# First-block decays spread by TensorE, arithmetic taken off GpSimd, raw weights held back

## The chip, the cores and the metric

One core of a Trainium2 chip runs the whole program. The metric is the time of one execution on the device in microseconds, the median over several runs. The profile is of one further execution.

## The reference

Three stages follow one another. The first is a chunked scan over 768 positions for 4 batches x 8 heads (head size 32, state size 16), in float32:

```python
for c in range(nc):
    cum = np.cumsum(la, axis=-1)                       # la = log(clip(a, 1e-6, 1))
    L = np.exp(cum[:, :, :, None] - cum[:, :, None, :]) * causal
    y_intra = np.einsum('bhij,bhjd->bhid', np.einsum('bhin,bhjn->bhij', Cc, Bc) * L, xc)
    y_inter = np.einsum('bhin,bhnd->bhid', Cc, state) * np.exp(cum)[:, :, :, None]
    y[:, :, sl] = y_intra + y_inter
    state = decay_full[:, :, None, None] * state + np.sum(Bx, axis=2)
```

Then come two MLPs over the 3072 tokens of width 256: an RMS norm and `silu(xn @ w_gate) * (xn @ w_val) @ w_out` with 1536 hidden columns, and `g @ w_out` with `h = x @ w_in`, `g = h * clip(h + 3, 0, 6) / 6` and 2048 hidden columns. The weights arrive as 64-bit floats.

## The kernel before

The tokens are cut into six blocks of 512. Stage A runs the first MLP over blocks j = 0 to 5 in twelve steps f each, stage B the second over six blocks in sixteen steps each. A step has a hidden part (`hidden`, products named hps), a gate on ACT, a product with it on DVE (`prod`, L793 or L795, which also frees the PSUM that the next hidden part needs), a split of the result into a high and a low part (`hi` on ACT, `lo`), and a result part (`result`, products named acc). Every matrix product is made of three products of rounded float32 operands (`mm3`, L752), 18 of 512 columns in a step of A and 12 in one of B. `lo` is a subtraction that runs on GpSimd (POOL) or DVE: `either` (L244) leaves the choice to the planner, and `two` (L247, instructions at L248) issues it.

The scan is done in 24 chunks k of 128 positions and one batch, in pairs q; block j needs the chunks 4j to 4j+3. For a pair, `load` (L341) brings `cb` (B, C, x), `L` (the decay factors, broadcast over 64 partitions) and `P` (their running products) in by DMA. `scan` (L400, DVE) makes the lower triangle of decays out of L, `bh` and `ch` scale B and C; PE makes scores (`score`, L426) and state updates (`grow`, L437); DVE multiplies scores by decays (`decay`, L480, tile SM), masks (`um`) and carries the state (V); PE makes y (`intra`, L451, and `inter`, L460). `finish_chunk` squares y and copies it out (ACT). The chunks of block 0 (pairs 0 and 1) come first; `norm_pair` (L557) then takes their means (PE, L537), a square root (ACT), a reciprocal and a Newton step (DVE), sends the result back through PE (L574), scales x and splits it into xh and xl. Later pairs are worked in `visit`s put between the steps of stage A at places given by `AT`; a visit does the front of a new pair and the back (y) of the one before it. `norm` (L612) does the same for later blocks, with a trip through DRAM (rnd, rb). For pair 0, L comes from the raw input and is clipped on DVE (L368); for the others it comes from `azero`, the clipped copy that `prefixes` (L300) writes to DRAM.

`weights` (L687) loads a raw weight tile, puts the two halves of its 64-bit numbers together (ACT L703 and L708, DVE `join` L712), and splits it into wh (ACT or DVE) and wl (POOL or DVE). Six raw buffers exist.

The order on every engine comes from `Plan` (L34): operations with a cost per engine, dependences, and a priority (the longest tail behind it plus a boost) are list-scheduled in model time, and the instructions are issued in that order. Each engine, and SP's queue of DMA issues, works in order. `Plan.run` also puts dummy products of zeros (`idle`, L310) into PE's gaps from the opening of the MLP's PSUM up to the first step.

Of the kernel before, what the change touches and what calls it, by code (L numbers as in the profile page):

```python
# [30 lines left out]
AT = [[2, 6, 8]] + [[0, 5, 6]] * 4  # L31


class Plan:  # L34
# [48 lines left out]
    def run(self):  # L83
# [32 lines left out]
        while len(out) < len(ops):  # L116
# [18 lines left out]
            if not now[e]:  # L135
# [4 lines left out]
            soon = min((r for r, s in future[e] if r < t + self.WAIT and s not in done  # L140
                        and -tail[s] - ops[s][4] < pri - self.MARGIN), default=None)
# [45 lines left out]
def block_kernel(ctx, tc, comb, ablk, w1, w2, cst, out):  # L187
# [8 lines left out]
    att, early, mlp = ExitStack(), ExitStack(), []  # L196
# [17 lines left out]
    rawx = [ap1.tile([128, 1536], F32, name=f"rawx{f}") for f in range(NRAW - 3)]  # L214

    P = Plan({"L": 2, "cb": 2, "P": 2, "ch": 4, "bh": 2, "SM": 4, "um": 4, "V": 6, "V1": 4,
              "S": 1, "S0": 1, "xT": 1, "sq": 1, "rn": 1, "rb": 1, "x": 2, "p": 3, "gh": 3,
# [8 lines left out]
    def dma(nbytes, n=1, e="DMA"):  # L226
        return {e: max(560 * n, nbytes // 300) if e == "DMA" else 560 * n, "bytes": nbytes}
# [4 lines left out]
    def d1(n):  # L232
        return 72 + 1.04 * n
# [10 lines left out]
    def either(n):  # L244
        return {"DVE": d1(n), "POOL": g1(n)}
# [14 lines left out]
    def setup():  # L260
        dve.memset(zero, 0.0)
        dve.memset(ones, 1.0)
        dve.memset(half, 0.5)
        pool.memset(eye8, 0.0)
# [54 lines left out]
    def place(k):  # L319
        return ("S0", 0) if 2 <= k < B else ("S", k // 2 - (k >= B))  # L320

    def bank4(k):
        p = ps_0 if 2 <= k < B else ps_at
        if p not in T:
            T[p] = p.tile([128, 4, 512], F32, name="sps")
        return T[p]
# [13 lines left out]

    def load(q):  # L341
        k0, bst = 2 * q, BOOST if 2 * q >= B else BOOST0 + (3000 if q == 0 else 0)
# [645 lines left out]
```

## Time and profile before

| | us |
|---|---|
| median of 3 runs (642.71 to 643.81) | 643.24 |
| the profiled execution | 643.43 |
| its span, first to last instruction | 641.6 |
| PE busy | 608.3 (95%) |
| DVE busy | 311.2 (49%) |
| ACT busy | 293.9 (46%) |
| POOL busy | 282.1 (44%) |

Busy times are unions of the instructions' durations; a matmul's record is longer than its distance to the next, since they are pipelined. Matmuls of plain float32 operands stand in the trace as two records each. An arrow in brackets names what ended an engine's idle time before an instruction.

### The profile page before, as it was taken

The page shows a single profiled execution, that of the slowest core. Times are in us where ns is not written, and L with a number is a line of the kernel's source. Part 1 is how long each engine was busy: PE and PEld are TensorE (multiplying, and loading weights), DVE is VectorE, ACT ScalarE, POOL GpSimd, SP SyncE. Part 2 cuts the span into 40 slices and gives each one's busy share as a digit, 9 for nine tenths or more (in the row PEclk, how much of TensorE's full clock was granted, in tenths as well). Part 3 has the DMA queues.
Part 4 walks back from the last instruction along what each step waited for, and adds up shares of the span by engine and source line. Part 5 has one row for each costly group of instructions (what it writes and reads, how often), then busy time and mean ns, then how long its engine had stood idle before and what let it go on. Part 6 is the DMA issues. An engine that isn't in the chain of part 4 may idle for free.

```text
span 641.6 us, 10828 instructions
## 1 busy us (share of the span) xinstructions
PE 608.3 (95%) x4414; PEld 491.9 (77%) x4414; DVE 311.2 (49%) x474; ACT 293.9 (46%) x484; POOL 282.1 (44%) x245
## 2 busy tenths in 40 slices
PE   1689999999999999999999999999999999999997
PEld 0567777778777777777888878788788787888886
DVE  4589975771683366255666422422424224222223
ACT  1368743232323233335766344545454454545443
POOL 3255373353334235233544344545455454544443
PEclk9999999999999999999999999999999999999999
DMA  7977314300340220022433000000000000000000
GB/s 254 313 241 287 102 32 129 105 18 1 100 111 7 79 79 17 3 83 76 140 131 113 0 1 0 1 33 2 1 34 1 0 34 1 5 29 1 33 1 33
DMA packets 15817, 42.18 MB, mean 66 GB/s; under 512 B 2116, under 2 KB 5400, under 8 KB 15768
## 3 DMA queue, kind: packets, MB, share of 16 engines
q1 hardware_dynamic: 15064, 39.63, 19.3%
q10 hardware_dynamic: 704, 1.87, 0.8%
q8 instruction: 34, 0.56, 0.4%
q14 instruction: 15, 0.12, 0.1%
HBM read 38.14 MB, written 3.35 MB: 65 GB/s over the span
## 4 chain that ended last, share of the span: by engine, by line
PE 78%; DVE 11%; DMA 5%; issue 4%; SPq 1%; ACT 0%; POOL 0%; DVEq 0%; POOLq 0%
PE hps L752 43%; PE acc L752 31%; DMA rb<-rnd 2%; DVE p L793 1%; DVE z L551 1%; DVE xT L648 1%; PE sps L451 1%; PE sps L460 1%; DVE xl L248 1%; DVE xh L254 1%; DVE yT L712 1%; DMA pref<-ac 1%; PE sps L426 1%; DVE y L552 1%; DMA rnd<-y 1%
## 5 line engine op out<-in xcount | busy, mean ns | idle before, releaser
L248 POOL TENSOR_TENSOR gl<-p,gh 128x512 fp32r<-128x512 f32 x161 | 215.5, 1338 | 300.0 <-ACT gh L800 279.7
L800 ACT CAST gh<-p 128x512 fp32r<-128x512 f32 x168 | 104.7, 623 | 117.2 <-PE acc L752 115.2
L795 DVE SCALAR_TENSOR_TENSOR p<-p,hps 128x512 f32<-128x512 f32 x96 | 65.9, 687 | 175.9 <-ACT p L787 175.8
L787 ACT ACTIVATE p<-hps,half 128x512 f32<-128x512 f32 x96 | 66.0, 687 | 76.9 <-POOL gl L248 76.2
L752 PE MATMUL hps<-xh,w1h 128*128 128x512 f32 x288 | 91.2, 398 | 4.4 <-DVE p L793 3.7
L752 PE MATMUL hps<-xh,w1l 128*128 128x512 f32 x288 | 89.4, 392 | 0.0
L752 PE MATMUL hps<-xl,w1h 128*128 128x512 f32 x288 | 89.2, 391 | 0.0
L793 DVE TENSOR_TENSOR p<-p,hps 128x512 f32<-128x512 f32 x72 | 49.1, 681 | 64.7 <-PE hps L752 56.3
L785 ACT ACTIVATE p<-hps 128x512 f32<-128x512 f32 x72 | 43.0, 598 | 79.4 <-POOL gl L248 66.2
L752 PE MATMUL acc<-gh,w2h 128*128 128x512 f32 x192 | 74.7, 389 | 0.0
L752 PE MATMUL acc<-gl,w2h 128*128 128x512 f32 x192 | 74.7, 389 | 0.0
L752 PE MATMUL acc<-gh,w2l 128*128 128x512 f32 x192 | 74.7, 389 | 0.0
L752 PEld LDWEIGHTS hps<-xh,w1h 128*128 128x128 f32 x288 | 53.1, 190 | 19.2 <-DVE p L793 6.8
L752 PEld LDWEIGHTS hps<-xh,w1l 128*128 128x128 f32 x288 | 54.4, 189 | 11.7
L752 PEld LDWEIGHTS hps<-xl,w1h 128*128 128x128 f32 x288 | 54.4, 189 | 11.6
L752 PE MATMUL hps<-xh,w2h 128*128 128x512 f32 x192 | 59.7, 392 | 2.1 <-DVE p L795 2.1
L752 PE MATMUL hps<-xh,w2l 128*128 128x512 f32 x192 | 59.2, 389 | 0.0
L752 PE MATMUL hps<-xl,w2h 128*128 128x512 f32 x192 | 59.1, 389 | 0.0
L752 PE MATMUL acc<-gh,w1h 128*128 128x512 f32 x144 | 57.4, 399 | 0.9 <-issue 0.9
L752 PE MATMUL acc<-gh,w1l 128*128 128x512 f32 x144 | 56.1, 390 | 0.0
L752 PE MATMUL acc<-gl,w1h 128*128 128x512 f32 x144 | 56.1, 390 | 0.0
L752 PEld LDWEIGHTS hps<-xh,w2h 128*128 128x128 f32 x192 | 35.6, 188 | 11.3 <-DVE p L795 4.3
(98 smaller groups left out, 710.4 us busy)
## 6 DMA issues: line engine op xcount, KB each, us to landing
cb<-comb SPq DMA_DIRECT2D x10, 896.0 KB
raw<-w SPq DMA_DIRECT2D x16, 512.0 KB
L<-azero SPq DMA_DIRECT2D x22, 256.0 KB
yT<-w SPq DMA_DIRECT2D x6, 768.0 KB
rawx<-w SPq DMA_DIRECT2D x6, 768.0 KB
out<-yT SPq DMA_DIRECT2D x12, 256.0 KB
P<-pref SPq DMA_DIRECT2D x24, 64.0 KB
rb<-rnd SPq DMA_DIRECT2D x5, 256.0 KB
```

Source lines behind the costliest of these rows:

```text
L248: eng[e].tensor_tensor(out=out, in0=a, in1=b, op=op)
L254: dve.tensor_copy(out, a)
L426: pe.matmul(out=o[64 * c:64 * c + 64, p], lhsT=cb[r, BN + c * SC:BN + (c + 1) * SC], rhs=cb[r, CP + c * CH:CP + (c + 1) * CH], start=True, ...
L451: pe.matmul(out=y[32 * g:32 * g + 32, 2 * t + c], rhs=SM[r, h], lhsT=cb[r, XX + D * h:XX + D * h + D], start=first, stop=True, skip_group_ ...
L460: pe.matmul(out=y[q:q + 64, p // 2 * 2 + c], lhsT=before(k, c)[r, :], rhs=T["ch", k][r, SC * c:SC * c + SC], start=False, stop=True, skip_ ...
L551: dve.tensor_tensor(out=z, in0=z, in1=y, op=ALU.mult)
L752: pe.matmul(out=o, lhsT=a, rhs=c, start=first and i == 0, stop=last and i == len(seq) - 1)
L785: act.activation(out=p[:, :n], in_=hid(hs[0])[:, :n], func=AF.Silu)
L787: act.activation(out=p[:, :n], in_=hid(hs[0])[:, :n], func=AF.Relu, scale=1.0 / 6.0, bias=half)
L793: dve.tensor_tensor(out=p, in0=p, in1=h, op=ALU.mult)
L795: dve.scalar_tensor_tensor(out=p, in0=p, scalar=1.0, in1=h, op0=ALU.min, op1=ALU.mult)
L800: act.copy(out=t[:, :n], in_=T["p", i][:, :n])
```

## The change

- The decays of chunks 0 to 3 no longer come by DMA. `ex` multiplies the clipped decays (96 rows, 256 columns) by stationaries of 128 columns that hold ones in one row pair (`pick`, copied on ACT out of the unit matrix); the product in PSUM (`Q`) is the broadcast, which the scan reads directly. `px` does the same for the running products of the second half chunk, which ACT copies into P (`back`). The raw decays for that arrive in a fifth group of columns of `ac`.
- Three products of zeros (`heat`: 512, 512 and 256 columns) stand first on PE; `idle` is now 512 columns wide and is put into gaps from the last mean of block 0 on.
- No subtraction or scaling goes to POOL: `either` names DVE alone.
- Raw weight f is held until another has landed: POOL copies one column into its buffer first, reading um of chunk 1 (f = 1) or an earlier raw weight (f from 2).
- Block 0's pairs are put in a new order: scores and updates of a pair together, y of both chunks in one piece (`first`), squares ahead of the means and copies behind; the root reads PSUM, xh is made in two parts. PSUM for pair 1 (`open0`) takes the banks of `Q` when all four scans have read them.
- The visits of blocks 0 and 1 are put at other steps (`VISITS`): pair 4 moves from block 0 to block 1, and pair 3's y stands alone.
- Up to the first step the planner waits longer for a more urgent operation (`calm`), and it takes DMA to run at 370 instead of 300 bytes per ns.

```diff
-AT = [[2, 6, 8]] + [[0, 5, 6]] * 4
+NWARM = (4, 4, 2)
+VISITS = {0: [(0, 2, None), (2, 3, 2), (6, None, 3), (8,)],
+          1: [(0, 4, None), (3, 5, 4), (6, 6, 5), (7,)]}
...
+            ahead, margin = self.WAIT, self.MARGIN
+            if i < self.calm:
+                ahead, margin = max(ahead, 0.6 * ops[i][0][e]), 1000
+            soon = min((r for r, s in future[e] if r < t + ahead and s not in done
+                        and -tail[s] - ops[s][4] < pri - margin), default=None)
...
-            t = 1 + next(s for s, i, _, _ in out if i == after)
+            t = 1 + max(s for s, i, _, _ in out if i in after)
...
+    ps_q = early[0].enter_context(tc.tile_pool(name="ps_q", bufs=1, space=PSUM))
+    Q = [ps_q.tile([128, 512], F32, name=f"spread{i}") for i in range(4)]
...
-        return {"DVE": d1(n), "POOL": g1(n)}
+        return {"DVE": d1(n)}
...
+        dve.memset(ac[:, 4], 1.0)
...
+    def four(t, n=4):
+        return t.rearrange("p (o n) -> p o n", o=1).to_broadcast([128, n, 128])
+
     def idle():
-        if "idle" not in T:
-            T["idle"] = mlp[0].tile([128, 512], F32, tag="acc0", name="idle")
-        pe.matmul(out=T["idle"][:, :128], lhsT=zero, rhs=zero, start=True, stop=True)
+        pe.matmul(out=bank4()[:, 0], lhsT=zero, rhs=four(zero), start=True, stop=True)
...
+    def heat(e):
+        for n in NWARM:
+            pe.matmul(out=Q[3][:, :128 * n], lhsT=zero, rhs=four(zero, n), start=True, stop=True)
+
+    spread = []
+
+    def broadcast():
+        def ex(e, k):
+            for u in range(2):
+                pe.matmul(out=Q[k][:, 256 * u:256 * u + 256], rhs=flat(az[:, :4]),
+                          lhsT=pick[:, 2 * k + u].rearrange("p c n -> p (c n)"),
+                          start=True, stop=True)
+
+        def px(e):
+            for k in range(B):
+                pe.matmul(out=Q[3][:, SC * k:SC * k + SC], rhs=ac[:32, 4],
+                          lhsT=eyeN[:, H * k:H * k + H].rearrange("p h n -> p (h n)"),
+                          start=True, stop=True, skip_group_check=True)
+
+        def back(e, q):
+            copy(e, tile2("P", q, [CH])[:, :, SC:],
+                 Q[3][:, 128 * q:128 * q + 128].rearrange("p (k i) -> p k i", i=SC))
+
+        def each(e):
+            act.copy(out=eyeN, in_=eye[:32, :32].rearrange("p (r n) -> p r n", n=1)
+                     .to_broadcast([32, 32, N]))
+
+        def spot(k):
+            for u in range(2):
+                r = 2 * k + u
+                act.copy(out=pick[:, r:r + 1], in_=eye[:96, :96].rearrange("p (c m o) -> p m c o", c=2, o=1)
+                         [:, r:r + 1].to_broadcast([96, 1, 2, SC]))
+
+        P.op({"ACT": 2 * a1(128)}, lambda e: spot(0), r=[("eye", 0)], w=[("raw", 4)], boost=4e5)
+        P.op({"ACT": 2 * a1(128)}, lambda e: spot(1), r=[("eye", 0)], w=[("pick", 1)], boost=3e5)
+        for k in (2, 3):
+            P.op({"ACT": 2 * a1(128)}, lambda e, k=k: spot(k), r=[("eye", 0)], w=[("pick", k)],
+                 boost=1e5)
+        P.op({"PE": 4500}, heat, w=[("hot", 0)], boost=1e9)
+        P.op({"ACT": a1(512)}, each, r=[("eye", 0)], w=[("raw", 5)], boost=2e5)
+        def some(k, bst):
+            P.op({"PE": 800}, lambda e, k=k: ex(e, k), w=[("Lp", k)],
+                 r=[("az", 0), ("raw", 4)] + ([("pick", k)] if k else []), boost=BOOST0 + bst, seq=[("Su", 0, 1)] if k == 3 else [])
+
+        some(0, 6000)
+        some(1, 6000)
+        P.op({"PE": 800}, px, r=[("ac", 0), ("raw", 5)], w=[("Lp", 3)], boost=BOOST0 + 5000)
+        for q in range(2):
+            P.op({"ACT": a1(128)}, lambda e, q=q: back(e, q), r=[("Lp", 3)], w=[("P", q)],
+                 boost=BOOST0 + 5000)
+        spread.append(lambda: [some(k, 0) for k in (2, 3)])
...
-                    in_=(azero if q else ablk)[c, k0:k0 + 2].rearrange("k m -> (k m)")
+                    in_=azero[c, k0:k0 + 2].rearrange("k m -> (k m)")
...
-        def clip(e, k):
-            t = T["L", k]
-            dve.tensor_scalar(out=t, in0=t, scalar1=1e-6, scalar2=1.0, op0=ALU.max, op1=ALU.min)
-            dve.memset(t[:, :, 0:1], 0.0)
-
-        seq = {1: [("P", 0)], 2: [("raw", 2)]}.get(q, [])
         cbs, Ls = [("cb", q, i) for i in range(2)], [("L", q, i) for i in range(2)]
+        seq = [("raw", 2)] if q == B // 2 else []
         if q == 0:
-            P.op(dma(98304), lambda e: nc.sync.dma_start(out=ac, in_=rows(ablk)), w=[("ac", 0)],
-                 boost=1e6)
-            P.op(dma(524288, 2), ld_L, w=Ls, boost=9e5)
-            for i in range(2):
-                P.op(dma(458752, 1, "ACT"), lambda e, i=i: ld_cb(e, i), w=[cbs[i]], boost=8e5)
+            P.op(dma(8192, 1, "ACT"), lambda e: act.dma_start(
+                out=ac[:32, 4], in_=ablk[1, :B].rearrange("k (h i) -> (k h) i", i=SC)),
+                w=[("ac", 1)], boost=2e6)
+            P.op(dma(98304), lambda e: nc.sync.dma_start(out=ac[:, :4], in_=rows(ablk)),
+                 w=[("ac", 0)], boost=1e6)
...
+            broadcast()
+        if q < B // 2:
+            for i, e in enumerate(("ACT", "DMA")):
+                P.op(dma(458752, 1, e), lambda e, i=i: ld_cb(e, i), w=[cbs[i]],
+                     boost=8e5 - 1e5 * q)
+        if q >= B // 2:
+            P.op(dma(524288, 2), ld_L, r=[("azero", 0)], w=Ls, boost=bst, seq=seq)
+            P.op(dma(917504), ld_cb2, w=cbs, boost=bst, seq=seq)
+            P.op(dma(131072, 2), ld_P, r=[("pref", 0), ("pref", 1)], w=[("P", q)], boost=bst)
 
 
         def scan(e, k):
+            if k < B:
+                tile2("L", q, [H, SC])
             L = flat(T["L", k])
-            dve.tensor_tensor_scan(out=L, data0=L, data1=flat(eye8), initial=0.0,
-                                   op0=ALU.mult, op1=ALU.add)
+            dve.tensor_tensor_scan(out=L, data0=Q[k] if k < B else L, data1=flat(eye8),
+                                   initial=0.0, op0=ALU.mult, op1=ALU.add)
...
+                 r=[("eye", 0), Ls[i] if k >= B else ("Lp", k)], w=[Ls[i]], boost=bst,
+                 seq=[("x", 0, 1, 2)] if q == B // 2 else [])
+            P.op(either(128) if k >= B else {"DVE": d1(128)}, lambda e, k=k: bh(e, k), r=[cbs[i], Ls[i]], w=[("bh", k)], boost=bst)
...
-            act.activation(out=rn(0)[2][:, k0:k0 + 2], in_=rn(0)[0][:, k0:k0 + 2], func=AF.Sqrt)
+            act.activation(out=rn(0)[2][:, k0:k0 + 2], in_=pair(k0)[:, :, 0], func=AF.Sqrt,
+                           scale=1.0 / DM, bias=eps)
...
-        def hi(e):
-            copy(e, parts()[0], T["xT", 0][:, :, cols])
+        def hi(e, t):
+            copy(e, parts()[0][:, t], T["xT", 0][:, t, cols])
...
+        if hold:
+            P.op({"POOL": 200}, lambda e: hold[0](raw(f)), r=hold[1], w=[kr], boost=soon, seq=seq)
...
+        P.op({"DVE": d1(cols)} if soon else either(cols), lo, r=[kt if wide else kr, kh], w=[kl],
+             boost=bst)
...
+    def open0(e):
+        early[0].close()
+        ps_0 = early[1].enter_context(tc.tile_pool(name="ps_0", bufs=1, space=PSUM))
+        T["ps", 1] = ps_0.tile([128, 4, 512], F32, name="sps0")
...
-            P.fill = idle, 225, opened[0], 4000, len(P.ops)
+            P.calm = len(P.ops)
+            P.fill = idle, 900, warm, 4000, len(P.ops)
...
+    def first(ks):
+        for k in ks:
+            intra(k)
+        pe.drain()
+        for k in ks:
+            inter(k)
+        pe.drain()
+
+    load(0)
     for q in range(2):
-        load(q)
-        for k in (2 * q, 2 * q + 1):
-            r, w = front_keys(k)
-            P.op({"PE": 700}, lambda e, k=k: score(k), r=r[:1], w=w[:1], boost=BOOST0)
-            P.op({"PE": 500}, lambda e, k=k: grow(k), r=r + w[:1], w=w[1:], boost=BOOST0)
+        ks = [2 * q, 2 * q + 1]
+        for k in ks:
+            rf, wf = front_keys(k)
+            P.op({"PE": 350}, lambda e, k=k: score(k), r=rf[:1] + [("open0", 0)][:q], w=wf[:1],
+                 boost=BOOST0 + 3000, seq=[] if q else [("Lp", k)])
+        for k in ks:
+            rf, wf = front_keys(k)
+            P.op({"PE": 250}, lambda e, k=k: grow(k), r=rf, w=wf[1:], boost=BOOST0 + 3000,
+                 seq=[("Sc", q, 1)])
+        if q == 0:
+            spread[0]()
+            load(1)
+            P.op({"HOST": 0}, open0, r=[("L", n, i) for n in range(2) for i in range(2)] +
+                 [("P", n) for n in range(2)], w=[("open0", 0)])
+    for q in range(2):
+        ks, r, w = [2 * q, 2 * q + 1], [], []
+        for k in ks:
             middle(k)
-        for k in (2 * q, 2 * q + 1):
-            r, w = back_keys(k)
-            P.op({"PE": 700}, lambda e, k=k: (intra(k), inter(k)), r=r, w=w, boost=BOOST0)
-            finish_chunk(k)
...
-        norm_pair(q, 0)
+            r, w = r + back_keys(k)[0], w + back_keys(k)[1]
+        P.op({"PE": 1500}, lambda e, ks=ks: first(ks), r=r, w=w, boost=BOOST0)
+        norm_pair(q, 0, [finish_chunk(k) for k in ks])
+    P.op({"HOST": 0}, open1, r=[("xT", 0, 2, t) for t in range(2)] + [("um", k) for k in (2, 3)],
+         w=[("open", 1)])
+    warm = last_mean[-1:]
...
+    def hold(f):
+        g = max(f - 2, 0) + (f == 2)
+
+        def go(t):
+            s = flat(T["um", 1]) if f == 1 else raw1(g)[:, 1:]
+            pool.tensor_copy(t[:, :1], s[:, :1])
+
+        return (go, [("um", 1) if f == 1 else ("raw", g)]) if f else ()
...
+                seq=[("azero", 0)], hold=hold(f))
+
+    def visit(q, o):
+        new, old = [[] if n is None else [2 * n, 2 * n + 1] for n in (q, o)]
...
-            if j == 0 and f == 0:
-                visit(B // 2)
-            if f in AT[j][:2]:
-                visit((j + 1) * B // 2 + 1 + AT[j].index(f))
-            if f == AT[j][2]:
+            n = 2 * j + 3
+            for v in VISITS.get(j, [(0, n, n - 1), (5, n + 1 if n + 1 < NK // 2 else None, n), (6,)]):
+                if v[0] == f and len(v) == 3:
+                    visit(*v[1:])
+            if f == VISITS.get(j, [(6,)])[-1][0]:
```

## Rows read from the trace of the kernel before

**Rows 1.** Windows: length, busy PE, PEld, DVE, ACT, POOL, clock, DMA share, GB/s.
```profile
7.00:37.00 30.00, 14.52 (x286) 11.42 (x287) 18.01 (x39) 11.89 (x22) 8.17 (x11) 1.00 0.97 291
37.00:91.00 54.00, 51.85 (x587) 40.40 (x587) 50.43 (x66) 37.74 (x60) 29.42 (x26) 1.00 0.49 170
91.00:148.00 57.00, 55.95 (x555) 44.77 (x554) 37.60 (x65) 17.04 (x31) 25.20 (x25) 1.00 0.25 75
```

**Rows 2.** Waits of PE from 40 us on: total us, times, longest.
```profile
PE hps L752 <- DVE p L793: 3.7, 7, 0.8
```

**Rows 3.** Timeline of the start, pair 0: start, us, engine, line, operation.
```profile
4.57 0.69 DVE L293 TENSOR_TENSOR_SCAN ac<-az,ah 96x256 f32<-96x256 f32 x1
...
12.93 0.69 DVE L480 TENSOR_TENSOR SM<-sps,L 128x512 f32<-128x512 f32 x1 [0.83 <-PE sps L437]
...
14.94 0.48 DVE L486 TENSOR_TENSOR um<-sps,gs 128x128 f32<-128x128 f32 x2
...
15.47 0.68 PE L451 MATMUL sps<-SM,cb 64*32 64x64 f32 x32 [1.24 <-DVE um L486]
...
17.11 0.49 PE L460 MATMUL sps<-ch,um 32*64 32x64 f32 x8
```

**Rows 4.** The same timeline, pair 1.
```profile
17.80 2.34 DVE L400 TENSOR_TENSOR_SCAN L<-L,eye 128x512 f32<-128x512 f32 x2 [1.13 <-DMA L<-azero]
...
27.36 0.49 PE L460 MATMUL sps<-ch,um 32*64 32x64 f32 x8
```

**Rows 5.** The same timeline, from y to the first product.
```profile
29.16 1.86 PE L537 MATMUL sps<-ones,sq 128*128 128x1 f32 x8 [0.17 <-ACT xT L252]
...
31.24 1.53 DVE L712 SCALAR_TENSOR_TENSOR yT<-yT 128x768 int32<-128x768 int32 x1
...
33.50 1.22 PE L574 MATMUL sps<-eye,y 128*128 128x128 f32 x4 [2.47 <-DVE y L552]
...
35.78 1.62 PE L313 MATMUL idle<-zero 128*128 128x128 f32 x6 [1.06 <-DVE xT L579]
...
37.05 1.20 PE L752 MATMUL hps<-xh,w1h 128*128 128x512 f32 x2
```

**Rows 6.** The same timeline, scores of a pair before and after the first product.
```profile
21.06 1.16 PE L426 MATMUL sps<-cb 32*64 32x128 f32 x32
...
41.32 0.69 PE L426 MATMUL sps<-cb 32*64 32x128 f32 x32
```

**Rows 7.** The same timeline, pairs of products of 512 columns.
```profile
38.05 1.05 PE L752 MATMUL hps<-xh,w1l 128*128 128x512 f32 x2
...
38.90 1.05 PE L752 MATMUL hps<-xl,w1h 128*128 128x512 f32 x2
...
44.29 0.62 PE L752 MATMUL hps<-xh,w1l 128*128 128x512 f32 x2
...
44.75 0.62 PE L752 MATMUL hps<-xl,w1h 128*128 128x512 f32 x2
```

**Rows 8.** The same timeline, DVE and POOL side by side.
```profile
43.57 4.44 DVE L400 TENSOR_TENSOR_SCAN L<-L,eye 128x512 f32<-128x512 f32 x2
...
44.18 2.75 POOL L248 TENSOR_TENSOR w1l<-yT,w1h 128x768 fp32r<-128x768 f32 x1
```

**Rows 9.** Groups: DVE 0 to 37 us; DVE, POOL 37 to 91: busy, mean ns.
```profile
L400 DVE TENSOR_TENSOR_SCAN L<-L,eye 128x512 f32<-128x512 f32 x5 | 5.9, 1210 | 1.2 <-DMA L<-azero 1.1
...
L400 DVE TENSOR_TENSOR_SCAN L<-L,eye 128x512 f32<-128x512 f32 x7 | 12.0, 1747 | 0.0
...
L248 POOL TENSOR_TENSOR gl<-p,gh 128x512 fp32r<-128x512 f32 x9 | 14.3, 1585 | 18.3 <-ACT gh L800 12.8 <-DVE w1l L248 5.5
L248 POOL TENSOR_TENSOR w1l<-yT,w1h 128x768 fp32r<-128x768 f32 x3 | 6.5, 2151 | 1.8 <-ACT w1h L252 1.8
L248 POOL TENSOR_TENSOR bh<-cb,L 128x128 f32<-128x128 f32 x7 | 5.4, 774 | 5.9 <-DVE L L400 5.9
```

**Rows 10.** Timeline, a subtraction of 512 columns on DVE by itself.
```profile
36.68 0.67 DVE L248 TENSOR_TENSOR xl<-xT,xh 128x512 fp32r<-128x512 f32 x1
```

More of the change, by code (lines that the diff above doesn't have):

```diff
@@ L226, in dma @@
     def dma(nbytes, n=1, e="DMA"):
-        return {e: max(560 * n, nbytes // 300) if e == "DMA" else 560 * n, "bytes": nbytes}
+        return {e: max(560 * n, nbytes // 370) if e == "DMA" else 560 * n, "bytes": nbytes}
     def a1(n):
@@ L341, in load @@
     def load(q):
[L342 removed]
+        k0, bst = 2 * q, BOOST if 2 * q >= B else BOOST0
         def ld_cb(e, i):
@@ L526, in finish_chunk, with out, pair @@
         P.op({"ACT": a1(256)}, square, r=[yk], w=[("sq", j, i)], boost=bst)
-        P.op({"ACT": a1(256), "DVE": d1(256)}, evac, r=[yk], w=[("xT", j, i)], boost=bst)
-    def place2(k):
-        return (2 + k % 2, 384) if k < B else (2, 384 + k % B)
+        def out():
+            P.op({"ACT": a1(256)} if k < B else {"ACT": a1(256), "DVE": d1(256)}, evac, r=[yk],
+                 w=[("xT", j, i)], boost=bst, seq=[("S0", k // 2, i) for i in range(2)] if k < B
+                 else [])
+        if k < B:
+            return out
+        out()
+    def pair(k):
+        return bank4(k)[:, 2:4, 384:]
     def mean(k):
-        j, i = k // B, k % B
-        bank, c = place2(k)
         for t in range(2):
-            pe.matmul(out=bank4(k)[:, bank, c:c + 1], lhsT=T["sq", j][:, t, i * CH:i * CH + CH],
+            pe.matmul(out=pair(k)[:, k % 2, 0:1], lhsT=T["sq", 0][:, t, k * CH:k * CH + CH],
                       rhs=ones[:, 0:1], start=t == 0, stop=t == 1, skip_group_check=True)
@@ L573, in back @@
             for k in (k0, k0 + 1):
-                pe.matmul(out=bank4(k)[:, 2 + k % 2, 384:512], rhs=eye, start=True, stop=True,
+                pe.matmul(out=pair(k0)[:, k % 2], rhs=eye, start=True, stop=True,
                           lhsT=rn(0)[1][:, k:k + 1].to_broadcast([128, 128]), skip_group_check=True)
@@ L579, in scale @@
             dve.scalar_tensor_tensor(out=x, in0=x, scalar=gs[:, t:t + 1],
[L580 removed]
+                                     in1=pair(k0), op0=ALU.mult, op1=ALU.mult)
         for k in (k0, k0 + 1):
[L583 to L586 removed]
+            last_mean.append(len(P.ops))
+            P.op({"PE": 300}, lambda e, k=k: mean(k), r=[("sq", 0, k)], w=[s[k % 2]], boost=bst,
+                 seq=[("Su", 1, 1)])
+        for f in rest:
+            f()
+        P.op({"DVE": 160}, shift, r=s, w=[v], boost=bst)
+        P.op({"ACT": 200}, root, r=s + [("table", 0)], w=[z], boost=bst)
+        P.op({"DVE": 180}, invert, r=[z, v], w=[y], boost=bst)
         newton(0, k0, k0 + 2, (v, y, z), bst)
[L588 removed]
+        P.op({"PE": 600}, back, r=[y], w=s, boost=bst)
         for t in range(2):
             P.op({"DVE": d1(256)}, lambda e, t=t: scale(e, t),
[L591 removed]
+                 r=[("xT", 0, k) for k in (k0, k0 + 1)] + s + [("cs", 0)],
                  w=[("xT", 0, k0, t)], boost=bst)
@@ L606, in norm_pair @@
         x = [("xT", 0, k0, t) for t in range(2)]
-        P.op({"ACT": a1(512), "DVE": d2(512)}, hi, r=x, w=[("x", b, q, 0)], boost=bst)
-        P.op({"DVE": d1(512)} if q else either(512), lo, r=x + [("x", b, q, 0)],
-             w=[("x", b, q, 1)], boost=bst)
+        for t in range(2):
+            P.op({"ACT": a1(256)}, lambda e, t=t: hi(e, t), r=x[t:t + 1], w=[("x", b, q, t)],
+                 boost=bst)
+        P.op({"DVE": d1(512)}, lo, r=x + [("x", b, q, t) for t in range(2)],
+             w=[("x", b, q, 2)], boost=bst)
     def norm(j, b):
-        bst, k0, s = BOOST, j * B, place(j * B + 2)
+        bst, k0, s = BOOST, j * B, ("Ss", j + 1)
         v, y, z = (("rn", j, n) for n in range(3))
         def sums():
-            return bank4(k0)[:, 2, 384:512]
+            return bank4()[:, 2, 384:512]
         def total(e):
@@ L649, in scale @@
                                      op0=ALU.mult, op1=ALU.mult)
-        P.op({"PE": 800}, total, r=[("sq", j, i) for i in range(B)], w=[s + (3, 0)], boost=bst)
-        P.op({"DVE": 290}, shift, r=[s + (3, 0)], w=[v], boost=bst)
+        P.op({"PE": 800}, total, r=[("sq", j, i) for i in range(B)], w=[s], boost=bst)
+        P.op({"DVE": 290}, shift, r=[s], w=[v], boost=bst)
         P.op({"DVE": 420}, guess, r=[v], w=[y, z], boost=bst)
@@ L685, in block_kernel, with weights @@
     wide = w1.dtype == mybir.dt.int64
-    def weights(tag, f, cols, src, raw, tmp, wh, wl, after=(), bst=0, soon=0, seq=()):
+    def weights(tag, f, cols, src, raw, tmp, wh, wl, after=(), bst=0, soon=0, seq=(), hold=()):
         kr, kt, kh, kl = ("raw" + tag, f), (("cv" if tag else "tmp"), f), ("wh" + tag, f), \
```

103 lines of the change are left out of this document (37 added, 66 removed).

## The prediction

> **What bounds the kernel now.** The windows by stretch come first: from 7 to 37 us PE is busy for 14.5 of 30 us, from 37 to 91 for 51.9 of 54, from 91 to 148 for 56 of 57 [rows 1]; only its idle or ill-used stretches can pay, and they lie at the start. The waits of PE after 40 us are small: the largest group, behind the DVE's product, has 3.7 us in seven waits [rows 2]. The timeline shows the first product of the MLP at 37.05 us [rows 5]; from there the kernel runs on products with short stops. The chain to 37.05: the prefix scan at 4.57; the scans of L wait for L by DMA; y of pair 0 complete at 17.11 + 0.49 = 17.6 [rows 3]; the scans of pair 1 at 17.80 behind a DMA again, its y complete at 27.36 + 0.49 = 27.85 [rows 4]; then means, norm, split and dummies for 9.2 us [rows 5]. The DMA engines are 97% busy from 7 to 37 us at 291 GB/s [rows 1], so every transfer in that chain is late.
>
> **Decays by TensorE.** Gone: four L transfers (1.05 MB), four P transfers (0.26 MB) and the two clips. 1.3 MB are 4.5 us of a full queue at 291 GB/s. Added: three heating products, and per chunk two of 256 columns. The price of fp32 columns: six records (three products of 128 columns) took from 35.78 to 37.05, 0.42 us per 128 columns [rows 5], at the slower pace. Heating has 10 x 128 columns: 4.2 us, from about 1.1 (zeros are ready) to 5.3; the clipped decays are there at 4.6 [rows 3], so heating may delay the first spread by 0.7. A chunk's spread has 4 x 128 columns: 1.7 us at the slower pace, 0.85 at the faster.
>
> Which pace? 32 score records took 1.16 us at 21 us and 0.69 at 41 us [rows 6], so scattered work ran slower. The granted clock reads 1.00 in all these stretches [rows 1], so the level must be read from spacing: pairs of 512-column products start 0.85 us apart at 38.05, which is 1.2 GHz, and 0.46 apart at 44.29 [rows 7], near 2.4 GHz. Rows alone thus leave both levels open for the spreads, as no row has heating ahead of scattered work. The Trainium skill (TensorE: Matmul & The Clock Gate, Part 1: The HAM clock gate) says that the half rate is the default, that activity releases it and that idling brings it back; this speaks against heating at 1 us, whose gain the idle gaps behind it would undo. By that rule the sum would end at the slow end below, near 637.5; were the heat to last, at the fast end, near 629.
>
> Fast end: spreads of chunks 0 and 1 by 7.1; on DVE from 6.3 two scans of 1.21 [rows 9], two bh of 0.2 (an estimate, from an um of equal size), two decays of 0.69, two um in 0.48 [rows 3], to 11.1; y of pair 0 (2.1 us, 15.47 to 17.6) by 13.0. The spreads of pair 1 run beside the decays, its scans 11.1 to 13.5; its scores must wait for both scans, as their PSUM banks are those that held the spreads; 0.7 of scores, then decays and um: 16.1; y at 17.8. Slow end: spreads at 7.0 and 8.7, second scan done at 10.0, scores and grows to 11.9, um at 12.6, y of pair 0 at 15.7; the last spread stands behind it in PE's queue and ends at 17.4, scan 18.7, scores 19.8, um 21.5, y 23.9. ACT's new copies (about 3 us) lie beside this, only the first pick near the path. I take 21.0, in the middle: DVE will also put the first weights and the norm of pair 0 into this chain. Against 27.85 that is 6.85 earlier.
>
> **From y to the first product**, 9.2 us now: 1.3 to the means, 1.86 of means, 2.5 to the back products (a weight join on DVE from 31.24 takes 1.5 of them), 2.3 to the dummies, 1.3 of dummies [rows 5]. After: squares go ahead of the copies (-0.7, with the means overlapped), the root reads PSUM itself and no join stands between (-1.3), hi goes in halves (-0.3). A dummy is four times as wide, 1.7 us at the slow pace; one behind the means and one behind the back products can overshoot (+0.3 net of the dummies of now). Sum 7.2, bounds 5.6 and 8. So the first product starts at 28.2: **-8.85**, bounds 23.4 (-13.6) and 31.9 (-5.1).
>
> **Clock at the first products.** The first three pairs took 1.00, 0.85 and about 0.85 us instead of 0.46 each [rows 5, 7], 1.3 us too much. Wider dummies from the last mean on: **-1.0**, between -1.3 and 0.
>
> **No arithmetic on GpSimd.** From 37 to 91 us DVE was busy 50.4 of 54 [rows 1]. It now gets nine lo of 0.67 (the price of an xl at 36.68 that stood alone [rows 10]), three weight lo, seven bh [rows 9] and a few smaller ones: about 12 us. In return it is freed of blocking: seven scans took 1.75 us each in this stretch against 1.21 before 37 us [rows 9], 3.8 us; V, xT and other two-input operations add, by a like ratio, some 6. One pair of rows shows how: two scans from 43.57 took 4.44 where 2.4 is their own, beside a POOL subtraction from 44.18 that took 2.75 [rows 8]: the second scan stood until POOL was through. The Trainium skill (SBUF — State Buffer, Who interferes with whom) has a DVE operation with two SBUF inputs and a GpSimd one that reads SBUF shut each other out for a whole instruction; the trace agrees (1.75 against 1.21). Net **0**, between -4 (the stops [rows 2] mostly go) and +5 (DVE runs full).
>
> **Visits.** Block 0 loses the front of pair 4: two scans, two decays, two um, two bh, four V, 5.5 us of DVE by the prices above, which is its slack for the line before. Its five transfers (1.57 MB, 5.4 us of the queue) leave SP's queue ahead of the weights and stand in block 1, where DVE is busy 37.6 of 57 us [rows 1] and hides them. No product is added; one visit is split, a restart more for PE: **+0.1**, bounds 0 and 0.6.
>
> **Weights held back.** Weight 1 waits on POOL for pair 0's um (11.1 to 12.6), the others for a weight before them to land. POOL does nothing else; on SP, the transfers of the next visit and later weights are queued behind the held ones, and PE waits for both. Weights 2 and 3 and the next visit's transfers (3.1 MB) go out at about 18 and need 10.7 us at 291 GB/s: landed at 28.7, converted by about 33.5; step 2 asks for weight 2 at 28.2 + 8 = 36. Hidden with 2.5 us to spare; if the first product comes at 23.4, late by 2. **+0.3**, bounds 0 and 4.
>
> The profiled execution took 643.43 us, 0.19 above the median of the runs, 643.24. 643.43 - 8.85 - 1.0 + 0 + 0.1 + 0.3 = 634.0; against the median **633.8**.
>
> **Rivals.** Forecast, 0.60: 629.5 to 638. *Weights late*, 0.13: the holds string transfers out and step 2 or 3 waits some 5 us; for it, DMA at 97% and SP in order; against it, 1.3 MB fewer to move: 639. *Stops vanish too*, 0.14: the start near its fast end and most stops behind DVE gone: 627 to 629.5. *Start no shorter*, 0.08: the spreads don't do what they are for; banks, picks and half clock hold pair 1's y near 27, and only norm and clock pay (-2, -1.0): 640.5, with late weights 643. *Slower*, 0.05: the product, which frees the PSUM of the next step, queues on DVE behind lo that POOL did before; the stops of up to 0.8 us [rows 2] spread into blocks 1 to 4, where DVE goes from 66% (37.6 of 57) to above 85%, against 93% in block 0, where they are now. It decides from 12 more stops (12 x 0.8 = 9.6, the gain); at 16: 647. Against it, 0.67 on DVE ends a lo sooner than POOL does.
>
> **Numbers.** A measurement of this kernel can tell 0.2% (1.3 us) from no change. Slower by more: the last rival, 0.05. Within it: a start no shorter with late weights, 0.03. Faster: 0.92. The range leaves out the last rival and the tails of the others: 627 to 641.
>
> **What would show it.** Right: no L or P transfer before the first product; scans that read PSUM from about 7 us; y of pair 1 near 21; the first MLP product near 28 and the next at full spacing; scans at 1.21 throughout. Wrong: a first product after 32, a wait of PE behind a weight conversion in steps 2 to 4, or waits behind the product above 10 us in sum.

## The result and the profile after

The changed kernel takes 628.98 us (median of 4 runs, 627.23 to 629.58) against 642.98 for the kernel before in the same rounds (4 runs, 642.58 to 643.81): a ratio of 0.9776, interval 0.9754 to 0.9798. The forecast was 633.8, range 627 to 641. The profiled execution is the fastest of the four, 627.23 us with a span of 625.2; that of before had 641.6, so 16.4 us are to be found. The medians differ by 14.0 only: the other three executions took 1.7 to 2.4 us longer, at a mean granted clock of 0.985 or 0.986 against 0.993, so what follows accounts for the fastest one.

The windows of the start of the kernel after (columns as in [rows 1]):

```profile
7.00:23.00 16.00, 12.50 (x328) 10.10 (x327) 12.56 (x30) 5.50 (x13) 0.67 (x4) 0.89 0.60 214
7.00:37.00 30.00, 25.55 (x371) 18.01 (x370) 24.05 (x52) 18.73 (x35) 2.24 (x7) 0.89 0.79 258
19.60:26.40 6.80, 6.56 (x29) 4.41 (x20) 4.30 (x14) 3.77 (x10) 0.70 (x2) 0.50 1.01 386
```

PE is busy for 25.6 of the 30 us from 7 to 37, where it was busy for 14.5 [rows 1]; the DMA share fell from 0.97 to 0.79. Behind the first product the two kernels are 10 us apart, so equal windows do not hold equal work. A block of stage A has 216 products of 512 columns; these are the windows of blocks 0 and 1, before and then after:

```profile
37.00:98.10 61.10, 58.95 (x618) 46.26 (x618) 55.46 (x78) 39.51 (x63) 33.55 (x29) 1.00 0.47 159
98.10:154.90 56.80, 55.75 (x554) 44.60 (x553) 33.26 (x53) 17.72 (x32) 23.64 (x23) 1.00 0.22 66
```

```profile
26.70:88.00 61.30, 57.61 (x553) 44.47 (x553) 57.34 (x101) 43.98 (x68) 2.89 (x6) 1.00 0.63 190
88.00:145.20 57.20, 56.42 (x617) 45.44 (x616) 39.46 (x85) 18.35 (x33) 0.00 (x0) 1.00 0.25 75
```

POOL loses nearly all of its 33.6 and 23.6 us. DVE's busy time grows by 1.9 us in block 0, to 57.3 of 61.3, though pair 4's front moved from there to block 1, and by 6.2 us in block 1. Block 0 itself is no shorter than before.

The timeline of the start (columns as in [rows 3]), from the heating products to the second weight:

```profile
1.05 4.63 PE L351 MATMUL spread<-zero 128*128 128x512 f32 x6 [1.05 <-DVE zero L270]
...
5.48 2.12 PE L358 MATMUL spread<-az,rawx 96*128 96x256 f32 x8
...
6.78 2.34 DVE L454 TENSOR_TENSOR_SCAN L<-spread,eye 128x512 f32<-128x512 f32 x2 [1.24 <-PE spread L358]
...
8.56 0.69 PE L481 MATMUL sps<-cb 32*64 32x128 f32 x32
...
13.68 0.86 PE L506 MATMUL sps<-SM,cb 64*32 64x64 f32 x64 [1.92 <-DVE um L540]
...
14.64 0.46 PE L515 MATMUL sps<-ch,um 32*64 32x64 f32 x16
...
18.08 0.18 POOL L975 COPY yT<-yT 128x1 f32<-128x1 f32 x1 [4.20 <-DMA yT<-w]
...
19.26 0.46 PE L515 MATMUL sps<-ch,um 32*64 32x64 f32 x16
...
26.74 0.83 PE L829 MATMUL hps<-xh,w1h 128*128 128x512 f32 x2
...
26.93 0.91 ACT L772 ACTIVATE yT<-yT 128x768 f32<-128x768 f32 x1
...
27.41 0.63 PE L829 MATMUL hps<-xh,w1l 128*128 128x512 f32 x2
...
27.88 0.66 PE L829 MATMUL hps<-xl,w1h 128*128 128x512 f32 x2
...
30.38 0.70 PE L829 MATMUL hps<-xh,w1h 128*128 128x512 f32 x2 [0.48 <-DVE w1h L263]
...
31.28 0.73 PE L829 MATMUL hps<-xh,w1l 128*128 128x512 f32 x2 [0.20 <-DVE w1l L257]
```

Of these lines none waits for a DMA before the weights. The scans read PSUM at 6.78; y of pair 0 is complete at 14.64 + 0.46 = 15.1 (17.6 before [rows 3]), that of pair 1 at 19.26 + 0.46 = 19.7 (27.85 before [rows 4]); the first product starts at 26.74 instead of 37.05 [rows 5], 10.3 us earlier.

The waits of PE from 22 us on (total us, times, longest), all that are listed:

```profile
PE sps L691 <- DVE um L540: 1.5, 3, 0.6
PE sps L506 <- DVE um L540: 1.5, 1, 1.5
PE hps L829 <- DVE p L870: 0.7, 2, 0.4
PE hps L829 <- DVE w1l L257: 0.5, 2, 0.3
PE hps L829 <- DVE w1h L263: 0.5, 1, 0.5
PE sps L481 <- DVE um L540: 0.4, 1, 0.4
```

The 3.7 us behind the DVE's product in seven waits [rows 2] have become 0.7 in two, in block 0. That row was not the whole list before: from 40 us on it has three more, the first of them behind the product of stage B.

```profile
PE hps L752 <- DVE p L795: 2.1, 5, 0.7
PE acc L752 <- issue: 0.9, 2, 0.5
PE hps L752 <- ACT p L785: 0.7, 2, 0.4
```

With [rows 2] that is 7.4 us, 6.2 of them after 65 us. And a listed wait is less than the stop it stands for, since a matmul's record is longer than its distance to the next. A fuller count goes over the starts of all 2448 products of 512 columns: the distance to the next, less the 0.227 us of products that follow each other at full clock, summed by what lies between. (Where a distance is too long by less than 0.02 us, the excess is counted with the stops after 65 us wherever it stands; up to there it comes to about 0.2 us.)

| PE time beyond back-to-back products, us | before | after | POOL off alone (below) |
|---|---|---|---|
| start of the first product | 37.05 | 26.74 | 38.38 |
| in the 3 us from there | 1.4 | 0.9 | 1.5 |
| stops later, up to 65 us | 2.0 | 2.3 | 1.9 |
| stops after 65 us | 12.0 | 1.4 | 2.9 |
| visits | 26.0 | 28.9 | 26.0 |
| totals of the norms (L691) | 3.5 | 5.3 | 3.5 |
| sum of the last five | 44.9 | 38.8 | 35.8 |

So 10.3 us come from the start, 10.6 from stops after 65 us, and 4.7 are given back in visits and totals; with the smaller terms (-0.5, +0.3, and less than 0.1 at the end) that is the 16.4.

### The profile page after: what moved, and what is told of

It is laid out like the page before. It is cut to its first block, busy times and chain, and to the rows that moved or that the text cites. A ratio compares the mean times of both kernels' runs of the same rounds, so it can differ in the third digit from the quotient of the medians.

```text
span 625.2 us, 10728 instructions
## 1 busy us (share of the span) xinstructions
PE 610.8 (98%) x4442; PEld 494.6 (79%) x4442; DVE 388.5 (62%) x703; ACT 297.3 (48%) x501; POOL 6.9 (1%) x21
## 4 chain that ended last, share of the span: by engine, by line
PE 91%; DVE 4%; DMA 3%; ACT 1%; issue 1%; SPq 0%; DVEq 0%
PE hps L829 48%; PE acc L829 36%; DMA cb<-comb 2%; DVE SM L534 1%; PE sps L506 1%; PE sps L481 1%; PE sps L515 1%; DMA P<-pref 1%; PE spread L351 1%; PE sps L492 1%; DVE L L454 1%; ACT sq L576 1%; PE sps L691 1%; PE spread L358 0%; DVE um L540 0%
## 5 line engine op out<-in xcount | busy, mean ns | idle before, releaser
L257 DVE TENSOR_TENSOR gl<-p,gh 128x512 fp32r<-128x512 f32 x168 | 115.5, 688 | 78.0 <-ACT gh L877 77.9
L829 PEld LDWEIGHTS acc<-gh,w2l 128*128 128x128 f32 x192 | 36.0, 188 | 7.5
```

What stands on the lines that cost most here:

```text
L257: eng[e].tensor_tensor(out=out, in0=a, in1=b, op=op)
L829: pe.matmul(out=o, lhsT=a, rhs=c, start=first and i == 0, stop=last and i == len(seq) - 1)
```

## The experiments

The first comparison asked what POOL's arithmetic is worth, inside the change and without it.

**POOL back (e1).** The kernel after, with the choice given back to the planner:

```diff
-        return {"DVE": d1(n)}
+        return {"DVE": d1(n), "POOL": g1(n)}
```

> The changed kernel with one thing undone: the planner may again put lo, bh and ch of later chunks on POOL. Theory (POOL's subtractions block two-input operations of DVE, and the late products this makes were PE's stops): the first product stays at 26.7 us within 0.7, scans after 37 us go back from 1.21 us to 1.5 or more on average, stops of about 0.6 us come back at the block boundaries of both stages, 4 to 7 us in sum, time near 634. Rival (the stops went because visits and steps stand in another order): scans may be slow again, but the boundaries stay without stops and the time within 1 us of 629.

Measured: 637.14 us, ratio 0.9890 (0.9866 to 0.9915), 8.2 above the kernel after (7.3 by the two ratios, which were taken in different rounds). The first product came at 26.36, so all of it lies behind. Of this kernel, the largest wait of PE from 40 us on (total, times, longest) and the group of the 20 scans from chunk 4 on (busy, mean ns, idle before):

```profile
PE acc L829 <- POOL gl L257: 3.5, 2, 1.9
...
L454 DVE TENSOR_TENSOR_SCAN L<-L,eye 128x512 f32<-128x512 f32 x20 | 32.2, 1639 | 2.0 <-DMA L<-azero 2.0
```

The 20 scans take 1.64 us each, against 1.21 in the kernel after, and the stops are back, but not only where the theory put them. In the count of the table they are 7.8 up to 65 us and 8.2 behind, against 2.3 and 1.4: nearly half of the new stops stand before 65 us, in block 0, where PE waits for low parts that POOL has not finished. The theory's direction holds; the size is above its bounds.

**POOL off alone (e2).** The kernel before, with DVE alone in `either` (the same edit reversed).

> The kernel before with one thing done: no arithmetic on POOL. Theory (blocking by POOL): 4 to 8 us faster than before, 635 to 639, the four boundary stops of stage B gone, scans at 1.21 us throughout, and the first product 1 to 2 us ahead of 37.05 as bh no longer waits on POOL. Rival (DVE becomes the bound once it has all the work): the waits of PE behind the product in the first block grow past 3 us and the time is 643 or more.

Measured: 635.85 us, ratio 0.9872 (0.9851 to 0.9892), 7.7 less. The first product came 1.3 us later, at 38.38, where 1 to 2 earlier was expected: in its trace PE does the back products of pair 0 (27.21, 1.22 us) ahead of the last y, which begins at 28.36 instead of 26.75, so the planner's order became another. All the gain lies behind it. The waits of PE after 40 us, all that are listed, and the group of scans from 37 to 91 us:

```profile
PE hps L752 <- ACT p L785: 0.6, 1, 0.6
```

```profile
L400 DVE TENSOR_TENSOR_SCAN L<-L,eye 128x512 f32<-128x512 f32 x7 | 8.2, 1208 | 0.0
```

One small wait is left of [rows 2], and the same seven scans that took 1747 ns [rows 9] take 1208. Stops after 65 us fall from 12.0 to 2.9 (last column of the table above).

**Which of POOL's work (e8, e9).** Two complements in the kernel before: in e8 `gl` goes to DVE and the rest may go to POOL, in e9 `gl` alone may go to POOL.

```diff
-        P.op(either(n), lo, r=[("p", i), ("gh", i)], w=[("gl", i)])
+        P.op({"DVE": d1(n)}, lo, r=[("p", i), ("gh", i)], w=[("gl", i)])
```

> The kernel before, with the low parts of the products (gl, 161 on GpSimd there) on DVE alone; weights' and x's low parts, bh and ch may still go to GpSimd. Theory: what GpSimd cost is gl, 215 of its 282 us: at the end of a block the last gl comes 0.65 us later from it than from DVE, and DVE's products, running beside gl, are shut out; then most of the 7.7 us of the run with GpSimd off come back: 636 to 637.5, the stops at block boundaries and in stage B gone, those of block 0 left. Rival: the cost is block 0, where DVE is full and weights, bh and ch on GpSimd shut it out: 640.5 to 642.

> The kernel before, with only gl free to go to GpSimd and every other low part, bh and ch on DVE: the complement. Theory: 641.5 to 643, scans still above 1.4 us, since gl alone shuts them out, and the stops at block boundaries as before. Rival: 636 to 638, with scans near 1.21.

Measured: e8 636.97 (0.9898, 0.9881 to 0.9914), 6.0 less than before; e9 641.38 (0.9973, 0.9963 to 0.9983), 1.6 less. In sum that is 7.6, against the 7.7 of e2. Stops after 65 us are 3.6 in e8 and 7.7 in e9, against 12.0 before. The scans of e8, then of e9:

```profile
L400 DVE TENSOR_TENSOR_SCAN L<-L,eye 128x512 f32<-128x512 f32 x24 | 30.6, 1286 | 1.2 <-DMA L<-azero 1.1
```

```profile
L400 DVE TENSOR_TENSOR_SCAN L<-L,eye 128x512 f32<-128x512 f32 x24 | 35.9, 1534 | 0.1
```

In time it was `gl`, four fifths of it, as the theory had it. The stops are not so cleanly split. The profiled executions, divided at the start of each block's products (us; e1's visit just at the start of block 1 is counted to block 1, where the kernel after has it):

| | first product | block 0 | blocks 1 to 5 | stage B |
|---|---|---|---|---|
| before | 37.05 | 61.1 | 274.8 | 264.5 |
| POOL off (e2) | 38.38 | 59.9 | 270.5 | 260.9 |
| `gl` off POOL (e8) | 37.42 | 61.0 | 271.2 | 260.9 |
| `gl` alone on POOL (e9) | 38.24 | 60.9 | 271.9 | 263.3 |
| after | 26.74 | 61.3 | 272.1 | 260.9 |
| after, POOL back (e1) | 26.36 | 67.3 | 272.2 | 264.6 |

In blocks 1 to 5 either edit alone gives most of e2's 4.3 us (3.6 and 2.9), so there most stops seem to need both kinds of POOL's work; in stage B e8 gives all of 3.6 and e9 a third. e9's small gain in time also has a first product 1.2 us later in it, and its stops are fewer than before, where its theory had them unchanged. Inside the change, POOL's work (e1) costs 6.0 us in block 0 and 3.7 in stage B, and next to nothing between.

How a stop comes about is seen at a block boundary of stage B in the timeline of the kernel before:

```profile
407.13 1.49 POOL L248 TENSOR_TENSOR xl<-yT,xh 128x512 fp32r<-128x512 f32 x1
407.22 0.69 ACT L787 ACTIVATE p<-hps,half 128x512 f32<-128x512 f32 x1 [0.26 <-POOL gl L248]
...
407.57 1.60 DVE L248 TENSOR_TENSOR xl<-yT,xh 128x512 fp32r<-128x512 f32 x1
...
409.08 0.39 PE L752 MATMUL acc<-gl,w2h 128*128 128x512 f32 x1
409.10 0.67 DVE L795 SCALAR_TENSOR_TENSOR p<-p,hps 128x512 f32<-128x512 f32 x1
...
409.82 0.73 PE L752 MATMUL hps<-xh,w2h 128*128 128x512 f32 x2 [0.36 <-DVE p L795]
```

The gate waited for POOL's `gl` and was ready at 407.91. DVE's own subtraction stood beside POOL's and took 1.60 instead of the 0.67 of [rows 10], so the product came at 409.10, and PE, due at 409.31 by the spacing above, started at 409.82: half a us. Both kinds of work are in it: in e9, where POOL has `gl` but not `xl`, the four stops like this one are 0.2 us each; in e8 they are gone. In the kernel after no stop between products is longer than 0.15 us after 42 us.

The next runs undo one part of the start each.

**Decays by DMA (e3).** The kernel after, heating and all, with L and P of the first four chunks loaded again, ahead of the raw weights, and no spreading:

```diff
+            P.op(dma(524288, 2), ld_L, r=[("azero", 0)], w=Ls, boost=19e4 - 1e4 * q)
+            P.op(dma(131072, 2), ld_P, r=[("pref", 0), ("pref", 1)], w=[("P", q)],
+                 boost=17e4 - 1e4 * q)
...
-            dve.tensor_tensor_scan(out=L, data0=Q[k] if k < B else L, data1=flat(eye8),
+            dve.tensor_tensor_scan(out=L, data0=L, data1=flat(eye8),
```

> The changed kernel with the decays of chunks 0 to 3 (L and P) brought in by DMA from the clipped copy, ahead of the raw weights, instead of by TensorE; heating, holds, norm and visits stay. Theory (the transfers are what made the start long): the scans wait for L until 11 us or later and for pair 1 until 14 or later, the first product is at 31 to 34 us, the time 633 to 636. Rival (the start is shorter because of the new order of norm and the held weights, and the spread is not needed): first product at 28.5 or earlier, time below 631.

Measured: 640.61 us, ratio 0.9947 (0.9926 to 0.9969). In its timeline:

```profile
13.96 2.34 DVE L448 TENSOR_TENSOR_SCAN L<-L,eye 128x512 f32<-128x512 f32 x2 [8.55 <-DMA L<-azero]
...
34.28 1.42 PE L823 MATMUL hps<-xh,w1h 128*128 128x512 f32 x2
```

The scans wait until 13.96 for a DMA, 7.2 us later than from PSUM, and the first product comes 7.5 later. In the profiled executions another 6.1 lie behind it (600.3 from the first to the last product, against 594.3), 3.4 of them in visits (32.3 against 28.9 in the class of the table). Both the first product and the time are above the theory's bounds, far from the rival's: without spreading the other changes leave 2.8 of the 10.3 us. The 7.5 hold more than the transfers, though. The granted clock was 0.50 from 9.05 to 36.36, so y and the norm went at half pace too; and L of pair 0 comes from the clipped copy here, while the kernel before loads it from the raw input and scans it from 9.77 on. A version that does that with the other changes was not run.

**No heating (e4).** The kernel after with `NWARM = ()`.

> The changed kernel without the three products of zeros at its start; everything else in the same order. Theory (the heating gives the spreads and scores the full pace until about 20 us): the spreads take 0.85 us per 512 columns of records more, the first product comes 1 to 2 us later (27.7 to 28.7), the time is 630 to 631. Rival (the heating only stands in the way of the first spread, which could start at 4.7): first product at 26.5 or earlier, time 628.5 or less.

Measured: 633.27 us, ratio 0.9832 (0.9805 to 0.9859), 4.3 above the kernel after (3.6 by the ratios). Timeline and a window:

```profile
4.78 3.78 PE L358 MATMUL spread<-az,rawx 96*128 96x256 f32 x8 [4.78 <-ACT rawx L379]
...
10.39 1.16 PE L481 MATMUL sps<-cb 32*64 32x128 f32 x32
...
32.00 1.20 PE L829 MATMUL hps<-xh,w1h 128*128 128x512 f32 x2
```

```profile
7.00:23.00 16.00, 14.64 (x240) 10.49 (x238) 10.22 (x21) 3.57 (x8) 0.49 (x3) 1.00 0.39 135
```

The spreads of two chunks start 0.7 earlier, take 3.78 instead of 2.12, and everything PE does up to y goes at that pace: the first product is 5.3 later. Heating is worth more than either theory gave it. The window says 1.00 while 32 scores take 1.16, as in [rows 6].

**The kernel after once more**, on the chip of the next three runs (e5 to e7) and in their rounds.

> The changed kernel once more, on the chip of the next three, so that differences near 1 us can be read. Every theory: 627 to 630, the first product at 26 to 27.5; the time goes with the moment at which the granted clock is back at full, near 26 us or some us later.

Measured: 627.89 us, ratio 0.9779 (0.9753 to 0.9806).

**Weights not held (e5).**

```diff
-                seq=[("azero", 0)], hold=hold(f))
+                seq=[("azero", 0)])
```

> The changed kernel without the holds: raw weights go out as soon as SP's order lets them. Theory (the holds are of little use once L and P are not transferred, and make weight 1 late): weight 1 is converted before the first product, the 1.7 us that PE waited for its halves at 29.5 to 33 go, first product within 1 us of 26.7, time 1 to 2 us better than the changed kernel. Rival (the early queue is still what the start waits for): the B and C transfers of pairs 0 and 1 land later, the first product comes at 28.5 or later, time 1 to 3 us worse.

Measured: 628.33 us, ratio 0.9773 (0.9757 to 0.9789): no difference to the kernel after. The waits for weight 1 are gone, but the clock falls sooner, and the first product comes at 27.49:

```profile
7.00:23.00 16.00, 13.33 (x324) 10.77 (x323) 11.64 (x29) 7.57 (x15) 0.00 (x0) 0.74 1.03 400
```

DMA runs full from 7 us (1.03, against 0.60), and the mean clock is 0.74 instead of 0.89. What was late at the weight is late at the start; neither theory had this. That the sooner fall (14.5 us, against 19.6) comes from the missing holds is not shown: in e1, which keeps them and has a DMA share of 0.68 from 7 to 23 us, the clock fell at 14.4.

**Visits as before (e6).**

```diff
-VISITS = {0: [(0, 2, None), (2, 3, 2), (6, None, 3), (8,)],
-          1: [(0, 4, None), (3, 5, 4), (6, 6, 5), (7,)]}
+VISITS = {0: [(0, 2, None), (2, 3, 2), (6, 4, 3), (8,)],
+          1: [(0, 5, 4), (5, 6, 5), (6,)]}
```

> The changed kernel with the visits of blocks 0 and 1 at their places of before (pair 4 in block 0, with the back of pair 3). Theory (DVE is full in block 0 and pair 4's front does not fit): PE's waits between the first product and 90 us grow from 5.5 us to 8 or more, time 2 to 4 us worse than the changed kernel. Rival (the place of the visits does not matter since DVE is no longer blocked): within 1 us of the changed kernel.

Measured: 630.41 us, ratio 0.9793 (0.9764 to 0.9821), 2.5 above the kernel after in the same rounds, but the intervals overlap: in time it is unclear. In the profiled execution (627.42) the visits cost 28.7 us, against 28.9: there the place makes no difference that shows.

**The gap at 12 us filled with zeros (e7).** Two more heating products behind the first pair's updates:

```diff
+    def more(e):
+        for n in (4, 4):
+            pe.matmul(out=Q[0][:, :128 * n], lhsT=zero, rhs=four(zero, n), start=True, stop=True)
...
+            P.op({"PE": 1700}, more, r=[("L", 0, 0)], w=[("hot", 1)], seq=[("Lp", 3)],
+                 boost=BOOST0 + 3000)
```

> The changed kernel with two more products of zeros of 512 columns in the idle gap of PE at 12.0 to 13.7 us. Theory (the fall of the granted clock at 19.6 us comes from that gap): the clock stays full past 19.6, the means and the products that send the roots back take 1.0 and 0.6 us instead of 1.7 and 1.2, the first product comes 1 to 1.5 us earlier (25.2 to 25.7), time 1 to 2 us better than the changed kernel and less spread between runs. Rival (the fall comes from the thin stretch of 14 to 20 us as a whole): clock falls near 19.6 all the same, first product within 0.5 us of 26.7.

Measured: 628.27 us, ratio 0.9773 (0.9758 to 0.9788): the same time. Timeline and a window:

```profile
11.94 1.88 PE L355 MATMUL spread<-zero 128*128 128x512 f32 x4
...
14.03 0.86 PE L510 MATMUL sps<-SM,cb 64*32 64x64 f32 x64 [0.20 <-DVE um L544]
```

```profile
20.00:27.00 7.00, 6.76 (x26) 4.41 (x20) 4.50 (x15) 4.02 (x11) 0.80 (x2) 0.52 0.99 385
```

PE's wait of 1.92 before y is 0.20 now, and the clock falls at 20.3 all the same. No run gave a version that beats the kernel after beyond the intervals.

## Why the prediction was right, and where it was not

The sign and the range held. The case that came is not the forecast's but the second rival, *stops vanish too* (627 to 629.5, chance 0.14): 628.98. That the range held is in part luck: two terms came out beyond their own bounds, on opposite sides (GpSimd below, visits above).

**Decays by TensorE**: right in mechanism. The start moved by 10.3, forecast 8.85, bounds 5.1 and 13.6. The miss is y of pair 1, taken at 21.0 and measured at 19.7; from there to the first product it took 7.0, forecast 7.2. The middle between the two paces was taken, and PE kept the fast one up to y (32 scores in 0.69). e3 and e4 undo one part each: without spreading the first product is 7.5 us later, without heating 5.3. The two overlap, since the clock fell early without spreading too. The Trainium skill (TensorE: Matmul & The Clock Gate, Part 1: The HAM clock gate) has activity release the half rate and idling bring it back. The trace agrees on the release: full clock, 2.4 GHz, from 5.9 us, behind 4.6 us of zeros. That the gaps would undo the gain did not come true: PE was idle for 1.9 us before y of pair 0, and that y still went at the fast pace.

**Clock at the first products**: right in the profiled execution, the one that has a trace. The second and third pairs start 0.67 and 0.47 us on; the loss is 0.2 instead of 1.3 to 1.4, a gain of 1.2 where 1.0 was forecast.

**No arithmetic on GpSimd**: this is the step that failed. It was put at net 0, between -4 and +5. By itself it is worth 7.7 (e2), inside the change 7 to 8 (e1), beyond the term's good end. Two things were wrong. The stops were priced from one row of the list of PE's waits [rows 2], 3.7 us; the whole list had 6.2 after 65 us alone, and by the distances of the products 12.0 us stood there. And the balance of DVE was drawn only from 37 to 91 us, most of block 0. There it was about right: in e2 the 33.6 us that POOL worked in block 0 are gone, DVE is busy there for 56.2 us instead of 55.5, and the block is 1.2 shorter. The gain lies in the blocks behind (4.3 in blocks 1 to 5, 3.6 in stage B), where DVE is far from full (33.3 of 56.8 us in block 1 before) and `gl` was on POOL at nearly each step. The mechanism itself stood in the prediction: the Trainium skill (SBUF — State Buffer, Who interferes with whom) has such a DVE operation and a GpSimd one exclude each other. The trace agrees: scans take 1.21 us without POOL, 1.29 with its small work, 1.53 with `gl`, and 1.64 with both (e1).

**Visits**: forecast +0.1; the class grew by 2.9, and the totals by 1.8. The price of moving and splitting was right (a front alone 1.1 and a y alone 1.5 make 2.6, as one visit does, and e6 has the same cost). What was missed is what is late next once the start is short. The chain that ended last (start, length, what) shows it in block 0:

```profile
26.89 13.58 DMA cb<-comb
...
40.49 4.95 DMA P<-pref
...
45.45 1.20 DVE L L454
...
51.16 0.60 DVE p L870
51.76 0.60 DVE gl L257
52.36 0.87 DVE w1l L257
...
53.43 0.63 DVE SM L534
...
54.76 0.29 DVE um L540
```

First come the inputs of the visits, to 45.4, then DVE's own queue: a scan, and behind the product `gl`, a weight's low part and the decays, until `um` at 54.76. The visit at 48.35 costs 3.3 instead of 2.6 and that at 54.55 3.7 instead of 1.5, with the wait of 1.5 for `um` in the list above. Of the two, e5 points to DVE: with the raw weights let go at once its chain that ended last is on DVE from 29.2 us on, and its visit still waits 1.9 for `um`. e1 does not part them: its visits cost 26.3, as before, but they stand 8 us later (56.59 and 63.43), behind waits for POOL. So some of "DVE runs full", the +5 end of the GpSimd term, probably came true here; in e2, with the later start, it does not (26.0). The three totals wait for an `um` for 1.5 in sum; they cost the same in e1 (5.3), so that is the new order, and why it puts them there was not tried.

**Weights held**: forecast +0.3, bounds 0 and 4. The stops from 29.5 to 33 us add up to 1.7, around the waits for weight 1 at 30.38 and 31.28 in the timeline above. It was not the transfer: POOL's copy that waits for weight 1 to land ran at 18.08, but ACT began to convert it only at 26.93, behind the norm. The later steps that the prediction feared for lost 0.5 at 41.3, behind a low part on DVE. Stops up to 65 us grew by only 0.3 in sum, as older stops of block 0 went. In the time the holds neither cost nor gain that shows (e5).

**The other rivals.** *Weights late* has its wait, at step 1 instead of 2 or 3, with a third of the 5 us. *Start no shorter* fell with the first product at 26.74. *Slower* fell with DVE's share of block 1, 39.5 of 57.2 us, far from the 85% that it needed: a low part takes DVE half of what it took POOL, and DVE got blocked time back.

In sum, against the 643.43 profiled: -10.3 (start), -1.2 (clock), -10.6 (stops after 65 us), +4.7 (visits and totals), +1.1 (the other stops, weight 1's the largest): 627.1; measured 627.23.

## What to carry to other kernels

Price the stops of the bounding engine from the starts of its own instructions over the whole span, not from a row of the list of waits: here 12 us stood after 65 us, where the whole list named half and the row that was used 2.5. Work moved from GpSimd to DVE can cost DVE far less than it took GpSimd (77 us against 275), since DVE does it faster and gets back the time in which it was shut out. And a shorter start meets what was hidden behind the long one: here the visits gave 2.9 us back, most likely to a DVE still full in block 0.

## What the runs showed of the hardware that was not expected

- The granted clock reads 1.00 until the profile's first record of a change: in e4 from 7 to 23 us, beside 32 scores in 1.16 us; at full clock they took 0.69. The level is to be read from spacing there; the slower kernel before has the higher mean clock by the profile.
- Wide products of zeros raised the clock, and it held for 13.7 us over work that left PE idle for a quarter of that (busy 10.4 of 13.7 from 5.9 to 19.6). Then it was 0.50 from 19.6 to 26.4, with PE busy for 6.56 of 6.8. Filling the gap at 12 us (e7) did not move the fall (20.3); running DMA full from 7 us, with the holds gone (e5), went with a fall at 14.5, but so did e1, with the holds and a DMA share of 0.70 from 5 to 14.4 us (14.4). What sets it stays open.
- A low part of 512 columns took 1.34 us on POOL and 0.69 on DVE. With POOL's 275 us of busy time gone (282.1 to 6.9), DVE's rose by 77 only (311.2 to 388.5), and PE's stops after 65 us fell by 9 (e2) to 11.
